# Letting the adding and the transposing transfers of a convolution and feed-forward kernel run beside each other

## The chip, the cores and the metric

One core of a Trainium2 chip runs the whole program. The metric is the device time of one execution, in microseconds (us).

## The reference, cut to what matters

Eight sequences of 4,224 tokens with 192 features pass through a convolution whose seven weights differ at each token and head, and then through a layer norm and a two-layer feed-forward net with a residual:

```
w   = softmax(weight_gen, over the 7 taps)            # per token and head (8 heads of 24 features)
y   = sum over k of w[..., k] * x[token - 6 + k]      # zeros ahead of the sequence
xn  = (y - mean(y)) / sqrt(var(y) + 1e-6) * g_ln
out = y + relu(xn @ w_ch1) @ w_ch2                    # 192 -> 768 -> 192
```

## The kernel before, in words

The tokens lie on 128 partitions and 264 columns; a column has 128 tokens, one to a partition. The work goes in chunks of four columns for the convolution (67 chunks, the first four of them otherwise) and in groups of four columns for the matrix products (66 groups).

**A chunk.** DVE multiplies x by the weights, `mul` (L544): three multiplications of two taps each into a buffer `pr` with two halves, and one of a single tap into `y`. Seven products have to be summed. Two of the six sums are left to the DMA engines: `dma_add` (L550) is issued by POOL and adds the second half of a `pr` buffer onto its first. The four others are `add` (L547) on POOL: two of them take the halves of the third buffer, and the last two, a2 and a3, take the results of the two adding transfers. There are 63 such chunks, so 126 adding transfers. Seven `pr` buffers exist, so a DVE multiplication can wait for an `add` that frees one.

**A group.** ACT sums, squares and scales the columns of `y` (L597, L602, L657) and rounds them to 16 bits (`hi`, L677). POOL makes the remainder (`lo`, L690). Both lie in one of two `hl` buffers. SP issues a transposing transfer, the *turn* (L694), into one of three `xT` buffers. PE multiplies it by the first matrix in three units of 36 matmuls (L712); each unit's result goes through ACT (`hh`, L727) and DVE (`hlo`, L729). PE then multiplies by the second matrix in two halves of 72 matmuls (L763). DVE adds the residual (L815) and SP stores (L823).

**SP's queue** also has the loads of x (L443) and of the weights (L449), and between the two output halves a step without work (the `hop`, L773) on which PE waits.

**The order.** Every operation has a place in one list, `PLACE`, written out by hand. `Plan.order` sorts by it, and each engine's instructions are issued in that order: what stands behind a waiting instruction of an engine waits too. `Plan.order` also keeps the last adding transfer and the last turn that it has met, and gives each adding transfer the last turn ahead of it as `behind`, and each turn the last adding transfer. At the end of the kernel function (L1014 to L1017) a wait is made of each `behind`: the instruction that issues the one transfer waits until the other has landed. `dma_add` waits on POOL, the turn on SP.

Of the kernel before, what the change touches and what calls it, by code (L numbers as in the profile page):

```python
# [238 lines left out]
class Plan:  # L239
# [32 lines left out]
    def order(self):  # L272
        out = sorted(self.ops, key=lambda o: o.place)
        tenant = {p: [None] * len(t) for p, t in self.pools.items()}
        done, last = set(), {"add": None, "turn": None}

        def freed(t):
            return -1 if t is None else max(x.place for x in t.ops)

        for o in out:  # L280
            assert o.deps <= done, "an operation is placed ahead of what it needs"
            for b in o.bufs:
                if b.slot is None:
                    b.slot = min(range(len(tenant[b.pool])), key=lambda i: freed(tenant[b.pool][i]))
                    assert freed(tenant[b.pool][b.slot]) < o.place, "no buffer is free"
                    tenant[b.pool][b.slot] = b
            if o.kind in last:
                o.behind, last[o.kind] = last["turn" if o.kind == "add" else "add"], o
            done.add(o)
        return out  # L290

# [2 lines left out]
def kernel(  # L294
# [30 lines left out]
    apart = mybir.DependencyInfo(mybir.DependencyClass.Sync, mybir.DependencyReason.DATA)  # L325
# [73 lines left out]
    for n in PARTS:  # L399
        pa = dict(S=s0, n=n, chunks=[], xT={})  # L400
        o = 0
# [611 lines left out]
    made = {}  # L1013
    for o in plan.order():  # L1014
        made[o] = o.fn()
        if o.behind:
            tc.add_manual_dep(made[o].ins, made[o.behind].ins.name, apart, reason="transfers kept apart")  # L1017


# [28 lines left out]
```

## Time and profile before

| | us |
|---|---|
| median of three runs | 856.57 (855.5 to 859.03) |
| the profiled execution | 856.96 |
| its span, first to last instruction | 855.2 |

PE is TensorE, PEld its weight loads, DVE VectorE, ACT ScalarE, POOL GpSimd, and SP the engine that only issues transfers. A name with q (SPq, POOLq) is the engine's sequencer, which waits and issues. In brackets at the end of a row stands the idle time ahead of an instruction and what ended it. All times in rows count from the start of the span.

### The profile page before, as it was taken

The page shows a single profiled execution, that of the slowest core. Times are in us where ns is not written, and L with a number is a line of the kernel's source. Part 1 is how long each engine was busy: PE and PEld are TensorE (multiplying, and loading weights), DVE is VectorE, ACT ScalarE, POOL GpSimd, SP SyncE. Part 2 cuts the span into 40 slices and gives each one's busy share as a digit, 9 for nine tenths or more (in the row PEclk, how much of TensorE's full clock was granted, in tenths as well). Part 3 has the DMA queues.
Part 4 walks back from the last instruction along what each step waited for, and adds up shares of the span by engine and source line. Part 5 has one row for each costly group of instructions (what it writes and reads, how often), then busy time and mean ns, then how long its engine had stood idle before and what let it go on. Part 6 is the DMA issues. An engine that isn't in the chain of part 4 may idle for free. (4 is left out here: it accounts for less than half of the span.)

```text
span 855.2 us, 37740 instructions
## 1 busy us (share of the span) xinstructions
PE 823.4 (96%) x16691; PEld 803.7 (94%) x16691; DVE 763.0 (89%) x863; ACT 646.1 (76%) x1797; POOL 728.7 (85%) x489
## 2 busy tenths in 40 slices
PE   4959999999999999999999999999999899999997
PEld 4548999999999999999999999999999899999997
DVE  7999999999999999999999999999999899673442
ACT  3888898787778888778869887878878678667521
POOL 7999999999899999999999889999986878964100
PEclk9979999999999999999999999999999999999999
DMA  9878878898878898788988799798876675845123
GB/s 219 192 176 171 166 153 186 162 199 192 188 169 198 192 190 162 181 164 189 203 187 203 163 184 197 165 168 198 190 152 151 159 137 134 158 80 108 37 74 94
DMA packets 146411, 140.91 MB, mean 165 GB/s; under 512 B 108487, under 2 KB 110415, under 8 KB 146247
## 3 DMA queue, kind: packets, MB, share of 16 engines
q1 hardware_dynamic: 127799, 88.95, 44.3%
q0 software_dynamic: 18144, 49.55, 31.3%
q8 instruction: 130, 2.13, 1.1%
q14 instruction: 34, 0.28, 0.1%
q10 hardware_dynamic: 304, 0.00, 0.0%
HBM read 36.43 MB, written 25.95 MB: 73 GB/s over the span
## 5 line engine op out<-in xcount | busy, mean ns | idle before, releaser
L547 POOL TENSOR_TENSOR y<-y,pr 128x768 f32<-128x768 f32 x252 | 514.2, 2206 | 15.4 <-DMA pr<-pr 6.1
L712 PE MATMUL ph<-xT,c_w 64*128 64x256 f16 x7128 | 417.0, 271 | 8.4 <-DVE hlo L729 8.0
L712 PEld LDWEIGHTS <-c_w 64*128 64x128 f16 x7128 | 383.8, 95 | 17.0 <-issue 11.1
L763 PE MATMUL po<-c_w2h,hh 64*128 64x192 f16 x3120 | 387.8, 243 | 0.8 <-SPq L773 0.4
L763 PE MATMUL po<-c_w2h,hlo 64*128 64x192 f16 x3120 | 387.8, 243 | 0.0
L763 PE MATMUL po<-c_w2l,hh 64*128 64x192 f16 x3120 | 387.7, 243 | 0.0
L544 DVE TENSOR_TENSOR pr<-x,wn 128x1536 f32<-128x1536 f32 (+1 forms) x193 | 332.1, 1738 | 5.5 <-POOL y L547 3.9
L763 PEld LDWEIGHTS <-hh 64*128 64x128 f16 x6240 | 307.2, 94 | 2.1 <-SPq L773 1.0
L729 DVE SCALAR_TENSOR_TENSOR hlo<-ph,hh 128x1024 f16<-128x1024 f32 x198 | 239.5, 1217 | 55.8 <-ACT hh L727 55.7
L727 ACT ACTIVATE hh<-ph 128x1024 f16<-128x1024 f32 x198 | 199.4, 1013 | 117.3 <-PE ph L712 114.8
L763 PEld LDWEIGHTS <-hlo 64*128 64x128 f16 x3120 | 175.3, 94 | 0.0
L690 POOL TENSOR_TENSOR hl<-xh,hl 128x768 f16<-128x768 f32 x66 | 132.8, 2031 | 33.3 <-ACT hl L677 33.2
L550 POOL DMA_DIRECT2D pr<-pr x126 | 130.1, 1233 | 27.4 <-DMA xT<-hl 14.4
L657 ACT ACTIVATE xh<-y,s 128x192 f32<-128x192 f32 x264 | 125.1, 535 | 22.1 <-DVE s L641 11.9
L602 ACT ACTIVATE junk<-y,s 128x192 f32<-128x192 f32 x264 | 116.1, 443 | 0.0
L597 ACT ACTIVATE junk<-y 128x192 f32<-128x192 f32 x264 | 92.2, 351 | 27.9 <-POOL y L547 27.5
L815 DVE SCALAR_TENSOR_TENSOR y<-po,c_fs,y 128x768 f32<-128x768 f32 (+1 forms) x66 | 65.7, 997 | 3.3 <-PE po L763 3.3
L544 DVE TENSOR_TENSOR y<-x,wn 128x768 f32<-128x768 f32 (+1 forms) x67 | 62.1, 933 | 0.2
L677 ACT ACTIVATE hl<-xh 128x768 f16<-128x768 f32 x66 | 55.0, 837 | 4.2 <-DMA xT<-hl 3.3
L602 ACT ACTIVATION_READ_ACCUMULATOR junk<-y,s 128x1 f32 x264 | 50.0, 189 | 0.0
L597 ACT ACTIVATION_READ_ACCUMULATOR junk<-y 128x1 f32 x264 | 49.8, 189 | 0.0
L469 POOL TENSOR_TENSOR e<-w,mx 128x672 f32<-128x672 f32 (+2 forms) x23 | 39.4, 1713 | 2.8 <-DVE mx L467 2.7
(75 smaller groups left out, 315.3 us busy)
## 6 DMA issues: line engine op xcount, KB each, us to landing
pr<-pr POOLq DMA_DIRECT2D x126, 384.0 KB, 6.2
x<-in_x_dram SPq DMA_DIRECT2D x65, 384.0 KB, 5.5
out_dram<-y SPq DMA_DIRECT2D x64, 384.0 KB, 4.4
w<-in_weight_gen_dram SPq DMA_DIRECT2D x21, 336.0 KB, 5.0
pr<-in_moe_w_ch_dram SPq DMA_DIRECT2D x2, 576.0 KB, 5.1
xT<-hl SPq DMA_TRANSPOSE x66, 3.6
hh<-in_moe_w_ch_dram SPq DMA_DIRECT2D x1, 768.0 KB, 10.1
out_dram<-y SPq DMA_DIRECT2D x4, 192.0 KB, 3.2
```

The lines of the kernel that those rows point to most:

```text
L544: E.tensor_tensor(out=ov, in0=xv, in1=wv, op=ALU.mult)
L547: Q.tensor_tensor(out=flat(0), in0=flat(0), in1=flat(k), op=ALU.add)
L550: return Q.dma_start(flat(to), flat(k), accum_op=ALU.add, max_dma_last_dim=CHUNK * D * 4)
L597: A.activation(junk[t % 2], at(y)[:, j, :], AF.Identity, scale=-1.0 / D, accum_out=at(s4)[:, 3, t : t + 1])
L602: A.activation(junk[2 + t % 2], at(y)[:, j, :], AF.Square, bias=at(s4)[:, 3, t : t + 1], accum_out=at(s4)[:, 0, t : t + 1])
L657: A.activation(paired(xh, t), at(y)[:, i, :].rearrange("p (c q) -> p c q", q=P // 2), AF.Identity, bias=at(s4)[:, 3, g + t : g + t + 1], s ...
L690: lambda xh=xh, hl=hl: Q.tensor_tensor(out=halves(hl, True), in0=pairs(xh), in1=halves(hl, False), op=ALU.subtract),
L712: T_.matmul(ph[:, r, v * 2 * P : (v + 1) * 2 * P], W["w1"][rows, WB[r][c], w, f : f + P], xv[rows, a, c, :, :], start=(v == 0 and k == 0), ...
L727: lambda: A.activation(at(hh)[:, us, :], at(ph), AF.Relu), [ph], [(hh, u)])
L729: lambda: V.scalar_tensor_tensor(out=at(hlo)[:, us, :], in0=at(ph), scalar=0.0, in1=at(hh)[:, us, :], op0=ALU.max, op1=ALU.subtract),
L763: made.append(T_.matmul(at(po)[:, z, e * D : (e + 1) * D], token(b, 2 * z + e, j)[rows], W[w][rows, j, :], start=(ph == 0 and e == 0 and k ...
L815: V.scalar_tensor_tensor(out=ysl, in0=at(po)[:, zs[0] : zs[-1] + 1, : 2 * D], scalar=W["fs"][:, 0:1], in1=ysl, op0=ALU.mult, op1=ALU.add)
```

## The change

`Plan.order` no longer records what an adding transfer or a turn stands behind, and the loop that issues the operations no longer makes a wait of it. Places, buffers, engines and all other waits stay.

```diff
-        done, last = set(), {"add": None, "turn": None}
+        done = set()
...
-            if o.kind in last:
-                o.behind, last[o.kind] = last["turn" if o.kind == "add" else "add"], o
             done.add(o)
...
         made[o] = o.fn()
-        if o.behind:
-            tc.add_manual_dep(made[o].ins, made[o.behind].ins.name, apart, reason="transfers kept apart")
```

## Rows read from the trace of the kernel before

**Rows 1.** The page, busy time of each engine over the span.
```profile
PE 823.4 (96%) x16691; PEld 803.7 (94%) x16691; DVE 763.0 (89%) x863; ACT 646.1 (76%) x1797; POOL 728.7 (85%) x489
```
**Rows 2.** Busy time by stretch (columns in the first line).
```profile
core 0: us, PE busy (x) PEld busy (x) DVE busy (x) ACT busy (x) POOL busy (x), PEclk, DMA share, GB/s
80.00:600.00 520.00, 518.27 (x10994) 512.30 (x10992) 512.24 (x560) 425.40 (x1200) 501.78 (x336) 1.00 0.85 181
...
640.00:660.00 20.00, 20.00 (x432) 20.00 (x429) 18.50 (x21) 15.80 (x46) 13.41 (x10) 1.00 0.62 134
660.00:680.00 20.00, 17.62 (x336) 16.90 (x332) 16.27 (x20) 12.27 (x32) 17.76 (x12) 0.91 0.66 154
680.00:740.00 60.00, 60.00 (x1280) 60.00 (x1278) 51.30 (x57) 47.84 (x135) 52.86 (x37) 1.00 0.73 154
740.00:760.00 20.00, 18.97 (x409) 18.76 (x405) 12.93 (x11) 13.74 (x38) 13.87 (x9) 1.00 0.49 81
```
**Rows 3.** The chain that ended last, 637 to 675 us: start, length, what.
```profile
637.86 4.70 DMA xT<-hl
642.56 0.02 issue
642.58 0.02 POOLq L550
642.60 0.50 issue
643.10 1.77 POOL pr L550 x2
644.86 1.15 POOL y L547
646.01 7.56 DMA pr<-pr
...
653.70 4.11 DMA xT<-hl
...
668.19 1.75 DVE pr L544
669.94 1.15 DVE hlo L729
671.09 0.04 issue
671.13 3.56 PE ph L712 x36
674.69 3.22 PE po L763 x72
```
**Rows 4.** The chain again, the same two pieces of PE's work later.
```profile
684.81 1.97 PE ph L712 x36
686.77 2.97 PE po L763 x72
```
**Rows 5.** Waits of SP's queue: for whom, us in total, times, longest.
```profile
SPq L694 <- DMA pr<-pr: 162.9, 34, 10.5
```
**Rows 6.** Waits of POOL over the whole span, the same columns.
```profile
POOL pr L550 <- DMA xT<-hl: 14.4, 9, 4.9
...
POOL y L547 <- DMA pr<-pr: 6.1, 8, 1.5
```
**Rows 7.** POOL in order of time, 643 to 661 us.
```profile
643.10 1.77 POOL L550 DMA_DIRECT2D pr<-pr  x2 [1.53 <-DMA xT<-hl]
644.24 2.46 POOL L547 TENSOR_TENSOR y<-y,pr 128x768 f32<-128x768 f32 x1
646.01 1.53 POOL L550 DMA_DIRECT2D pr<-pr  x1
646.79 6.39 POOL L547 TENSOR_TENSOR y<-y,pr 128x768 f32<-128x768 f32 x3
658.09 0.87 POOL L550 DMA_DIRECT2D pr<-pr  x1 [4.91 <-DMA xT<-hl]
```
**Rows 8.** DVE in order of time, the wait at 668 us.
```profile
668.19 1.75 DVE L544 TENSOR_TENSOR pr<-x,wn 128x1536 f32<-128x1536 f32 x1 [2.17 <-POOL y L547]
```
**Rows 9.** POOL in order of time, the adding transfers issued at 726 us.
```profile
725.99 3.57 POOL L550 DMA_DIRECT2D pr<-pr  x4 [1.68 <-DMA xT<-hl]
```
**Rows 10.** ACT in order of time, the wait at 745 us.
```profile
745.36 0.36 ACT L597 ACTIVATE junk<-y 128x192 f32<-128x192 f32 x1 [3.29 <-POOL y L547]
```
**Rows 11.** The turn's line, L694: time to landing.
```profile
DMA to landing us min/median/max: 3.2/3.6/6.5
```
**Rows 12.** The adding transfer's line, L550: time to landing.
```profile
DMA to landing us min/median/max: 3.8/6.2/10.7
```
**Rows 13.** Waits of PE between 80 and 855 us.
```profile
PE ph L712 <- DVE hlo L729: 4.1, 5, 2.3
PE po L763 <- SPq L773: 0.4, 1, 0.4
PE po L763 <- DVE y L815: 0.2, 1, 0.2
```
**Rows 14.** The turn's stretch on SP and its `lo` on POOL, in order of time.
```profile
645.06 0.60 SPq L823 DMA_DIRECT2D out_dram<-y  x1
653.70 1.43 SPq L694 DMA_TRANSPOSE xT<-hl  x1
...
634.41 1.97 POOL L690 TENSOR_TENSOR hl<-xh,hl 128x768 f16<-128x768 f32 x1
```

## The prediction

> **What bounds the kernel now.** I read four views in turn. The page's busy times name PE: 823.4 of 855.2 us [rows 1]. The split by stretch says when: from 80 to 600 us PE is idle 520 - 518.27 = 1.7 us, and DVE (512.24) and POOL (501.78) are nearly as full [rows 2]. So nothing that the transfers do there can give back more than 1.7 us. Of the stretches listed after that, PE has a hole in two: 20 - 17.62 = 2.4 us between 660 and 680, and 20 - 18.97 = 1.0 us between 740 and 760 [rows 2]. PE's own waits agree: 4.1 us behind DVE's `hlo`, the longest 2.3, and never for a transposed tile [rows 13]. A turn that lands earlier is therefore worth nothing to PE directly; it can only pay by way of POOL, ACT or SP.
>
> The chain of waits shows what is behind the first hole. Its links between 637 and 658 us are a turn (4.70 us), two POOL issues, an adding transfer (7.56), a turn (4.11): each transfer is issued just after the other kind has landed [rows 3]. One round of this loop is 653.70 - 637.86 = 15.8 us. PE needs for a group three units of 1.97 and two halves of 2.97 [rows 4], 11.9 us. For this round the alternation is slower than PE, while the DMA engines were busy only 0.62 of the stretch [rows 2]: it is the waiting from landing to issue that costs, not the bytes.
>
> The hole costs more than its 2.4 us. After it PE ran a unit in 3.56 us and a half in 3.22 [rows 3] where it takes 1.97 and 2.97 otherwise [rows 4]: 1.8 us more. The granted clock of that stretch reads 0.91 [rows 2], and 9% of 20 us is the same 1.8 us. Together the hole is 4.2 us.
>
> **The change, part by part.** Nothing is added and no instruction moves; two sets of waits go.
>
> *The wait of POOL's issue on a turn.* It ended 14.4 us of idle time, in 9 places [rows 6]. The two in the loop are 1.53 and 4.91 us [rows 7]. Without them POOL would be up to 6.4 us earlier at 658 us. From the end of the POOL work at 646.79 + 6.39 = 653.2 the issue at 658.09 could follow at once [rows 7]. What POOL's lateness did is in DVE's row: a multiplication stood 2.17 us for a buffer that an `add` had to free, and `hlo`, one place behind it, was the instruction that PE waited for [rows 8, 3]. 4.91 is more than twice 2.17, so I take this wait away whole, and with it PE's 2.4 us and the 1.8 us of slow clock that followed. What is late next is ACT's rounding and POOL's `lo` between the two; the margin of 4.91 - 2.17 = 2.7 us is what they may use up.
>
> *The same wait at 726 us* is 1.68 us, ahead of four issues [rows 9]. POOL is then busy until 745 us, where ACT stands 3.29 us for POOL's sum [rows 10], and PE's hole of 1.0 us follows. 1.68 covers 1.0. Here I am less sure, since PE arrives 4.2 us sooner; but ACT's and DVE's orders hold PE's evictions too, so that most of the work before this point moves forward with PE. I take 1.0.
>
> *The wait of a turn on an adding transfer.* SP stood 162.9 us in 34 of 66 turns [rows 5]. Most of this is no loss: a turn also needs its `lo`, and PE never waited for the tile [rows 13]. The turn at 653.70 shows how far one can come forward: its `lo` ended at 636.4, SP's store ahead of it was issued by 645.7 [rows 14], so it could go 8 us earlier. Behind a turn in SP's queue stand loads, stores and the hop; PE's wait on the hop is 0.4 us in all [rows 13]. I book nothing for this part. What hides it is PE's full row and the three `xT` buffers.
>
> *What the transfers cost each other.* The waits that go kept every turn of this trace apart from every adding transfer, so this price isn't in it. The nearest rows are the spreads of the times to landing, in which a transfer shares the DMA engines with others: a turn takes 3.2 to 6.5 us [rows 11], an adding one 3.8 to 10.7 [rows 12]. Per overlapped pair I bound the extra by 0 below (a gain by meeting is excluded, as both draw on the same engines) and by 6.5 - 3.2 = 3.3 us above. Who would pay? PE has no wait for a turn. POOL's `add` waited for an adding transfer in 8 places, 6.1 us [rows 6]: in these a later landing counts in full. 8 x 3.3 = 26.4 us is the upper end, against 14.4 us of waits that go. I take the lower end for the forecast, near the medians, 3.6 and 6.2, that lie close to the minima and which the loads and stores in the same queues already disturb. Both ends are kept for the range.
>
> A rule bears on this. Rows first: the DMA share was 0.85 on average from 80 to 600 us and 0.62 in the stretch of the loop [rows 2]. The Trainium skill (DMA: Bandwidth & Descriptors, Rules for kernel authors) says that transfers issued from SP, ACT and POOL run on the same 16 DMA engines and interleave, so that several issuing engines save issue time and bring no bandwidth. By that rule overlapping would only stretch each transfer, and the sum would be 0. By the rows there is idle time to fill in the loop, and the sum stays 5.2.
>
> **The sum.** 2.4 + 1.8 + 1.0 = 5.2 us off the profiled 856.96 gives **851.8 us**. The median shown is 0.4 us below the profiled execution, which I leave in the range. 0.5% of the median, about what a measurement of this kernel can tell from no change, is 4.3 us, so the limit is 852.3: the forecast is only just beyond it.
>
> **The rivals.**
>
> *No change, as the shared engines give it back* (about 855.5). The freed transfers stretch each other, POOL waits for its adding transfers where it waited for turns, and the hole at 671 us stays or moves. For it: 4.91 us of relief become 4.91 - 3.3 = 1.6 if one pair overlaps at the upper price, less than the 2.17 that DVE stood; the round is then still too long, and about 1 us of PE's idle time goes without the clock. That is the skill's rule as a mechanism. Against it: the share of 0.62. A weaker form, that the change removes waits that other waits hold anyway, is true of the 32 turns that SP did not hold back [rows 5] but not of the loop, where no other release stands within microseconds [rows 7, 14].
>
> *Slower: POOL becomes late all along* (about 863). The place is `add` a2 and a3, directly behind the landing of an adding transfer. The price is up to 3.3 us per place, in 8 places 26.4 us; less the 14.4 us freed, 12 us net. POOL is busy 501.78 of 520 us between 80 and 600 [rows 2], so it can make up little; about half would reach PE, with further drops of its clock: 857 + 6 = 863, and 869 if all does. It decides from 14.4 / 8 = 1.8 us per place on, which is below the upper price. For it: POOL's small reserve. Against it: the tight places number 8 of 126, and not each has a turn beside it.
>
> *Faster than forecast* (about 850): also the 1.7 us of 80 to 600 us go. 856.96 - 6.9 = 850.1 is the floor that PE's work allows.
>
> **How the numbers follow.** The forecast gets 0.38 and its faster neighbour 0.06, together 0.44 faster by over 0.5%. No change gets 0.33; what lies between (one hole gone, the clock's share not) belongs to it. The slower case gets 0.23. The range begins at 848.5, the floor less the 1.5 us by which runs of one kernel lie under the profiled one (855.5 against 856.96), and goes up to 863, the slower case at half pass-through, which leaves out its upper end and little else. The likeliest case alone spans 850 to 853.
>
> **What would show it.** Right: the times to landing of both kinds rise by under 2 us; POOL has no idle time behind turns, and SP none behind adding transfers; PE is busy through 660 to 680 us with the granted clock at 1.00; DVE's wait for POOL there is under 0.5 us. Wrong: POOL's `add` waits for adding transfers for over 20 us in all; or the hole returns later with another name ahead of `hlo`; or times to landing of 10 us and more become the rule.

## The result, and the profile after

The changed kernel takes 849.28 us (median of four runs, 849.1 to 851.12) against 857.56 for the kernel before (855.5 to 859.03): a ratio of 0.991, 95% interval 0.9883 to 0.9937. The profiled execution took 849.11 us, its span 847.3. The lines moved up by two: the turn is L692, the adding transfer L548, `add` L545, `lo` L688, PE's products L710 and L761.

The page's busy times, and the split by stretch (columns as in [rows 2]):

```profile
PE 819.4 (97%) x16691; PEld 802.9 (95%) x16691; DVE 762.4 (90%) x863; ACT 646.1 (76%) x1797; POOL 727.5 (86%) x489
```
```profile
80.00:600.00 520.00, 519.39 (x11044) 515.43 (x11042) 514.23 (x562) 426.67 (x1201) 503.47 (x337) 1.00 0.87 182
640.00:660.00 20.00, 20.00 (x440) 19.99 (x436) 19.50 (x27) 16.81 (x47) 15.83 (x12) 1.00 0.93 175
660.00:680.00 20.00, 20.00 (x424) 20.00 (x420) 18.66 (x19) 16.68 (x49) 17.12 (x12) 1.00 0.77 168
740.00:760.00 20.00, 20.00 (x433) 20.00 (x430) 15.29 (x13) 13.88 (x36) 11.47 (x9) 1.00 0.39 63
```

Both holes are gone, the granted clock reads 1.00 between 660 and 680 us, and in the stretch of the loop the DMA share rose from 0.62 [rows 2] to 0.93; the engines moved 175 GB/s there, where it was 134.

What POOL and SP's queue wait for now (first column who, then for whom, us in total, times, longest):

```profile
POOL pr L548 <- DVE pr L542: 13.6, 7, 4.1
...
POOL y L545 <- DMA pr<-pr: 1.6, 2, 1.1
```
```profile
SPq L692 <- POOL hl L688: 107.4, 32, 9.7
```

No issue of POOL waits for a turn any more (14.4 us in [rows 6]), and POOL's `add` stood for adding transfers for 1.6 us, not 6.1. SP's turn still waits, now for its `lo`. POOL has become early and waits for DVE instead.

Where did the time come from? PE's order is the same in both kernels, so each block of its products can be compared by its start. First PE's timeline of the kernel before, then of the changed one (start, length, engine, line, count; x72 are two units, and a block that runs past the queried stretch shows a smaller count):

```profile
661.80 4.11 PE L712 MATMUL ph<-xT,c_w 64*128 64x256 f16 x72
...
677.73 1.49 PE L712 MATMUL ph<-xT,c_w 64*128 64x256 f16 x24
...
749.95 2.28 PE L712 MATMUL ph<-xT,c_w 64*128 64x256 f16 x38 [1.03 <-DVE hlo L729]
...
850.63 0.25 PE L792 MATMUL ph<-c_w2h,hlo 128*128 128x192 f16 x1
```
```profile
659.30 4.11 PE L710 MATMUL ph<-xT,c_w 64*128 64x256 f16 x72
...
666.20 2.14 PE L710 MATMUL ph<-xT,c_w 64*128 64x256 f16 x36
...
671.14 1.05 PE L710 MATMUL ph<-xT,c_w 64*128 64x256 f16 x16
...
742.14 4.11 PE L710 MATMUL ph<-xT,c_w 64*128 64x256 f16 x72
...
842.80 0.25 PE L790 MATMUL ph<-c_w2h,hlo 128*128 128x192 f16 x1
```

At the first block PE is 661.80 - 659.30 = 2.5 us ahead, collected in steps of 0.2 to 0.6 us since 80 us; at 600 us it was 2.1. The next unit began at 671.13 before [rows 3] and at 666.20 after: 4.9 us ahead. The next block is free of the slow clock too, and starts at 671.14 where it was 677.73: 6.6 us ahead. At 749.95 against 742.14 the lead is 7.8 us, and there it stays to the end (850.63 against 842.80). So the 7.8 us are 2.5 early, 4.1 at the first hole with its clock, 1.2 at the second.

The times to landing, the turn's first, then the adding transfer's:

```profile
DMA to landing us min/median/max: 3.2/4.7/6.7
```
```profile
DMA to landing us min/median/max: 3.8/6.1/10.7
```

The median turn takes 1.1 us longer than in [rows 11]; the adding transfer takes 0.1 us less [rows 12].

### The profile page after: what moved, and what is told of

It is laid out like the page before. It is cut to its first block, busy times and chain, and to the rows that moved or that the text cites. A ratio compares the mean times of both kernels' runs of the same rounds, so it can differ in the third digit from the quotient of the medians.

```text
span 847.3 us, 37725 instructions
## 1 busy us (share of the span) xinstructions
PE 819.4 (97%) x16691; PEld 802.9 (95%) x16691; DVE 762.4 (90%) x863; ACT 646.1 (76%) x1797; POOL 727.5 (86%) x489
## 4 chain that ended last, share of the span: by engine, by line
PE 58%; DVE 10%; POOL 3%; issue 2%; ACT 1%; DMA 1%; SPq 0%; DVEq 0%; POOLq 0%
PE po L761 29%; PE ph L710 29%; DVE pr L542 5%; DVE hlo L727 3%; POOL y L545 2%; DVE y L542 1%; DVE y L813 1%; PE ph L790 1%; POOL pr L548 1%; DMA out_dram<-y 1%; ACT junk L600 0%; DVE wn L496 0%; ACT junk L595 0%; ACT hh L725 0%; POOL hl L688 0%
## 5 line engine op out<-in xcount | busy, mean ns | idle before, releaser
L545 POOL TENSOR_TENSOR y<-y,pr 128x768 f32<-128x768 f32 x252 | 505.4, 2157 | 13.9 <-DVE y L542 5.9
L710 PE MATMUL ph<-xT,c_w 64*128 64x256 f16 x7128 | 415.1, 270 | 5.0 <-DVE hlo L727 4.9
L710 PEld LDWEIGHTS <-c_w 64*128 64x128 f16 x7128 | 383.6, 94 | 11.0 <-issue 6.7
L761 PE MATMUL po<-c_w2h,hh 64*128 64x192 f16 x3120 | 387.6, 243 | 0.1
L761 PE MATMUL po<-c_w2l,hh 64*128 64x192 f16 x3120 | 387.7, 243 | 0.0
L761 PE MATMUL po<-c_w2h,hlo 64*128 64x192 f16 x3120 | 387.6, 243 | 0.0
L761 PEld LDWEIGHTS <-hh 64*128 64x128 f16 x6240 | 306.9, 94 | 0.7 <-SPq L771 0.3
L761 PEld LDWEIGHTS <-hlo 64*128 64x128 f16 x3120 | 174.9, 94 | 0.0
L688 POOL TENSOR_TENSOR hl<-xh,hl 128x768 f16<-128x768 f32 x66 | 126.7, 1938 | 40.2 <-ACT hl L675 38.1
L548 POOL DMA_DIRECT2D pr<-pr x126 | 127.7, 1194 | 15.3 <-DVE pr L542 13.6
## 6 DMA issues: line engine op xcount, KB each, us to landing
hh<-in_moe_w_ch_dram SPq DMA_DIRECT2D x1, 768.0 KB, 10.3
```

What stands on the lines that cost most here:

```text
L545: Q.tensor_tensor(out=flat(0), in0=flat(0), in1=flat(k), op=ALU.add)
L548: return Q.dma_start(flat(to), flat(k), accum_op=ALU.add, max_dma_last_dim=CHUNK * D * 4)
L688: lambda xh=xh, hl=hl: Q.tensor_tensor(out=halves(hl, True), in0=pairs(xh), in1=halves(hl, False), op=ALU.subtract),
L710: T_.matmul(ph[:, r, v * 2 * P : (v + 1) * 2 * P], W["w1"][rows, WB[r][c], w, f : f + P], xv[rows, a, c, :, :], start=(v == 0 and k == 0), ...
L761: made.append(T_.matmul(at(po)[:, z, e * D : (e + 1) * D], token(b, 2 * z + e, j)[rows], W[w][rows, j, :], start=(ph == 0 and e == 0 and k ...
```

## The experiments

The first four kernels put one part of the waits back. Each is the kernel before with one more condition at the place where the waits are made; they ran on one chip, beside 24 runs of the kernel before (median 856.23). The changed kernel ran in a job of its own; the medians of the kernel before differ by up to 1.3 us between jobs, and times compared across them are that uncertain.

**Only the turn's wait stays; POOL issues freely.**

```diff
-        if o.behind:
+        if o.behind and o.kind == "turn":
```

> The adding transfers no longer wait for turns; each turn still waits for the adding transfer ahead of it. Loop theory (the holes came from transfers that waited for each other in a ring, and cutting either side of it opens the ring): at least 5 of the 8 us come, 849 to 852 us, PE full from 660 to 680 us. Rival (POOL's 14.4 us of waits alone were the cost): the whole gain comes, 849 to 850. Second rival (the freed turns are what pays): 855 or more.

Measured: 849.34 us (849.1 to 849.46), ratio 0.9922 (0.9901 to 0.9943). The whole gain is there, though SP still stands for adding transfers and PE waits for next to nothing between 80 us and the end:

```profile
SPq L694 <- DMA pr<-pr: 122.0, 32, 10.4
```
```profile
PE ph L712 <- DVE hlo L729: 0.5, 2, 0.3
```

**Only the adding transfer's wait stays; SP issues turns freely.**

```diff
-        if o.behind:
+        if o.behind and o.kind == "add":
```

> The turns no longer wait for adding transfers; each adding transfer still waits for the turn ahead of it on POOL. Loop theory: a turn that starts up to 8 us sooner has landed before POOL asks for it, so the ring is open too and 849 to 852 us result, with under 6 us of POOL's waits on turns left of 14.4. Rival (POOL's waits alone were the cost, and they stay): 855 or more. Second rival (the freed turns are what pays): 849 to 850.

Measured: 854.37 us (853.07 to 857.52). The median is 1.9 us lower, but the ratio, 0.9992 (0.9976 to 1.0009), can't be told from no change. The loop theory fell for the whole time: it wanted 849 to 852, and under 6 us of waits. The first rival's 855 is missed by 0.6 us. POOL kept 10.3 of its 14.4 us of waits on turns. POOL's waits in total, POOL's issues in order of time up to the wait at 655 us, SP's timeline of that stretch, the time to landing of the two turns issued between 640 and 662 us, and the stretch in which the kernel before has its first hole:

```profile
POOL pr L550 <- DMA xT<-hl: 10.3, 6, 3.9
```
```profile
641.73 1.77 POOL L550 DMA_DIRECT2D pr<-pr  x2 [0.33 <-issue]
...
644.64 1.54 POOL L550 DMA_DIRECT2D pr<-pr  x1
...
655.74 0.87 POOL L550 DMA_DIRECT2D pr<-pr  x1 [3.93 <-DMA xT<-hl]
```
```profile
645.69 0.60 SPq L823 DMA_DIRECT2D out_dram<-y  x1
646.46 4.38 SPq L694 DMA_TRANSPOSE xT<-hl  x1
```
```profile
DMA to landing us min/median/max: 7.1/8.0/9.0
```
```profile
660.00:680.00 20.00, 20.00 (x433) 20.00 (x430) 18.62 (x22) 15.22 (x40) 16.70 (x11) 1.00 0.86 176
```

The turn does go 7.2 us sooner (646.46, before 653.70 [rows 14]), as soon as the store ahead of it was issued. But the adding transfers that POOL issued at 641.7 and 644.6 are in flight, and it lands after 9.0 us instead of 4.1 [rows 3]: of the 7.2 us, 4.9 are given back in flight. The other 2.3 us reach POOL, whose issue comes at 655.74 instead of 658.09 [rows 7]. With that the first hole is gone: in this execution (853.83 us) PE is full from 660 to 680 us and keeps its clock.

So the first hole is not where this kernel loses its time. It loses it in other places. At 551.84 us PE stood 1.47 us for the hop (0.45 at the same product before), after POOL's `add` had stood 2.40 us (0.58 before) for an adding transfer that took 9.6 us with a turn in flight (7.8 before). Between 680 and 740 us PE is idle for 0.5 us, and the second hole is there with 0.9 us.

**Both waits go, but only late.**

```diff
-        if o.behind:
+        if o.behind and o.place < 2168:
```

> Waits of both directions are gone from place 2168 on (from about 615 us), and stay ahead of it. If the two holes at 671 and 749 us were made by the waits beside them: 4.1 + 1.2 = 5.3 us of the 7.8 us by which PE's work ends sooner in the changed kernel come, 851.5 to 853.5 us. Rival (lateness collected before 615 us decided the holes): 855 or more.

Measured: 850.64 us (849.81 to 853.05), ratio 0.9941 (0.992 to 0.9961): 1.4 us over the fully changed kernel, and 1.3 over the one above in which POOL issues freely. In its profiled execution PE is busy for the whole of 660 to 680 and of 740 to 760 us, so most of the gain belongs to the waits beside the holes. The time is 0.9 us below the expected range; the early waits cost 1.4 us here and not the 2.5 us of the profiled pair.

**Both waits go, but only early.**

```diff
-        if o.behind:
+        if o.behind and o.place >= 2168:
```

> Waits of both directions are gone up to place 2167 (about 615 us), and stay from there on. If the holes were made by the waits beside them, both stay and only the 2.2 us come by which PE was ahead at 621 us in the changed kernel: 854.5 to 856. Rival (lateness collected before decided the holes): the first hole goes with them, 850 to 852.

Measured: 853.4 us (851.93 to 856.72), ratio 0.9976 (0.996 to 0.9993). This lies between the two expectations. The second hole stays, with 0.9 us of idle time between 740 and 760 us. Of the first, little is left:

```profile
660.00:680.00 20.00, 19.53 (x410) 19.14 (x406) 17.84 (x18) 14.96 (x42) 15.72 (x11) 1.00 0.68 163
```

PE is idle 0.5 us here, not 2.4 [rows 2], and keeps its clock. Nor is it the same place: the unit that had to wait at 671.13 us before starts at 666.94 without a wait, and PE stands 0.42 us two units later, at 679.60. So lateness from before 615 us counts: without it, the waits of the loop no longer make the first hole. By the kernel with late waits freed, lateness without these waits doesn't make it either. The two gains, 5.6 us there and 2.8 here in the same job, add up to more than the 6.9 us of the kernel in which POOL issues freely, as they would if each takes the first hole away.

**The waits put back for the loop alone.**

```diff
-        if o.behind:
+        if o.behind and 2168 <= o.place <= 2330:
```

> The changed kernel with the waits of both directions put back for the transfers at places 2168 to 2330 alone (some 615 to 670 us), 13 of 192. If POOL's waits on turns there make the first hole: it comes back, 851 to 854 us, with POOL idle behind turns for 3 to 8 us. Rival (the hole needs the lateness of the waits before it too): 849 to 850, no change from the changed kernel.

Measured: 852.57 us (850.69 to 855.35, ten runs; before 856.66 in the same job), ratio 0.9954 (0.9936 to 0.9973). The waits of these transfers (15 by the list, ten adding ones and five turns, not the 13 that the expectation names) cost 3.3 us over the changed kernel by the medians. The profiled execution is the fastest of the ten, and in it POOL has two waits on turns there, 7.6 us, within the expected 3 to 8. POOL's two issues and, below them, the stretch of the first hole:

```profile
653.89 0.88 POOL L550 DMA_DIRECT2D pr<-pr  x1 [4.79 <-DMA xT<-hl]
...
666.78 0.88 POOL L550 DMA_DIRECT2D pr<-pr  x1 [2.80 <-DMA xT<-hl]
```
```profile
660.00:680.00 20.00, 19.53 (x410) 19.14 (x406) 17.83 (x18) 14.55 (x40) 15.32 (x10) 1.00 0.78 165
```

The hole itself did not come back as expected, though. As with the early waits freed, PE doesn't wait at the unit of 671.13 us (666.95 here) and stands 0.42 us two units later, with its clock kept. This execution took 850.69 us, 1.9 less than the median, and what PE did in the other nine isn't known. The second hole, beside which no wait was put back, is gone (20.00 of 20 us between 740 and 760).

**No wait, but POOL made late by other work.** The changed kernel with memsets of a scratch tile, which nobody reads, ahead of five adding transfers:

```diff
     made = {}
+    late = {2195: 2, 2238: 1, 2292: 5, 2502: 2, 2565: 1}
     for o in plan.order():
+        for _ in range(late.get(o.place, 0)):
+            Q.memset(scratch, 0.0)
         made[o] = o.fn()
```

> The changed kernel, without any wait between the two kinds, but with memsets of a scratch tile on POOL (about 1 us each, 11 in all) ahead of five adding transfers at which POOL had stood for turns in the kernel before (places 2195, 2238, 2292, 2502, 2565; 10.7 us there). If POOL's lateness in itself makes the holes, whoever makes it late: they come back in part, 851 to 855 us. Rival (the hole needs transfers that meet or wait): 849 to 850.

Measured: 853.92 us (852.91 to 855.51), ratio 0.9961 (0.9935 to 0.9988): 4.6 us over the changed kernel. POOL's timeline, PE's, and the stretch of the first hole:

```profile
650.15 5.53 POOL L1016 MEMSET scratch<- 128x1152 f32 x5
655.62 0.88 POOL L549 DMA_DIRECT2D pr<-pr  x1
```
```profile
668.69 2.14 PE L711 MATMUL ph<-xT,c_w 64*128 64x256 f16 x36 [1.85 <-DVE hlo L728]
```
```profile
660.00:680.00 20.00, 18.02 (x376) 17.66 (x372) 16.13 (x15) 12.92 (x36) 15.54 (x11) 1.00 0.97 163
```

The hole is back at the same unit, ended by the same `hlo`, and no transfer had waited for one of the other kind. DVE stood 2.5 us for POOL's `add` on the way, as it did before for 2.17 [rows 8]. The slow clock did not come back: PE was idle for 2.0 us and the granted clock reads 1.00.

So it is POOL's lateness that makes the hole, whatever makes POOL late. The profiled executions also say how late: what counts is POOL's issue (the one at 658.09 us before) against PE's own progress, for which the start of PE's block at 661.80 us can stand.

| kernel | POOL's issue, us | PE's block, us | issue ahead of block | PE stands at the next unit |
|---|---|---|---|---|
| before | 658.09 | 661.80 | 3.7 | 2.26 |
| changed, with memsets | 655.62 | 659.76 | 4.1 | 1.85 |
| waits in the loop alone | 653.89 | 660.01 | 6.1 | 0 |
| only early waits gone | 653.88 | 660.01 | 6.1 | 0 |
| only SP free | 655.74 | 662.14 | 6.4 | 0 |
| changed | 648.09 | 659.30 | 11.2 | 0 |

The memsets bring POOL's issue 0.4 us earlier against PE than before, and the hole is 0.4 us shorter; where the issue is 2.4 us earlier or more, there is no hole at this unit. A wait of 4.8 us in the loop shows at PE or not, by how late POOL already is.

**The price of meeting, by itself.** A kernel of transfers alone, of the sizes and forms used here, run once: ten rounds each of the five combinations, each round behind the landing of the one before. In its text the combinations are:

```python
((add_alone,), (turn_alone,), (add_first, add_second), (add_beside, turn_beside_one),
 (add_first_beside, add_second_beside, turn_beside_two))
```

> No convolution and no feed-forward: ten rounds each of an adding transfer alone, a turn alone, two adding transfers, an adding transfer beside a turn, and two beside a turn, each round behind the landing of the one before; one tile is stored. The times to landing are what counts. If the engines interleave and share: beside one another each takes 1 to 2 us longer than alone (adding about 4, turn about 3.2 us alone). Rival (the transfers fit beside each other at no price): within 0.3 us of alone. Third way (the transposing one is held up far more): over 6.5 us for the turn.

Times to landing of the single rounds, in this order: adding alone, turn alone, adding beside a turn, the turn beside it.

```profile
DMA to landing us min/median/max: 3.9/3.9/4.1
...
DMA to landing us min/median/max: 3.6/3.7/3.7
...
DMA to landing us min/median/max: 5.2/5.7/5.8
...
DMA to landing us min/median/max: 4.7/5.3/5.8
```

And of the rounds with two adding transfers: the first and the second without a turn, the first and the second beside a turn, and that turn.

```profile
DMA to landing us min/median/max: 3.9/3.9/4.0
...
DMA to landing us min/median/max: 5.5/5.5/5.5
...
DMA to landing us min/median/max: 5.2/5.2/5.6
...
DMA to landing us min/median/max: 6.7/6.7/7.0
...
DMA to landing us min/median/max: 4.8/5.1/5.5
```

By the medians each kind pays 1.2 to 1.8 us for the other: 5.7 - 3.9 and 5.3 - 3.7 in the pair; 5.2 - 3.9, 6.7 - 5.5 and 5.1 - 3.7 in the three. It is the first of the three ways expected. The price is for bare pairs and threes; with the kernel's other transfers about, the one freed turn above paid 4.9 us (9.0 against 4.1). Still, one behind the other a pair lands after 3.9 + 3.7 = 7.6 us, and beside each other both are there after 5.7.

## Why the prediction was right, point by point

**The holes: right in place and size, and in the cause with one thing missing.** 4.2 us were booked for the first with its clock, 4.1 came; 1.0 for the second, 1.2 came. That POOL's lateness makes them is shown from two sides: without its waits on turns they go though the turns still wait, and with memsets in their place both return (2.0 us idle at the first, 0.9 at the second). What the prediction left out is the lateness that POOL brings into the loop: with the wait of 4.8 us put back in the loop and no waits ahead of it, PE did not stand at that unit in the profiled execution. And the 1.8 us of slow clock, booked as a consequence of the hole, followed it in the profiled execution of the kernel before alone; the hole of 2.0 us under memsets came with the granted clock at 1.00. How often the clock's part is lost isn't known. The signs listed for "right" are in the trace: the median landings rose by 1.1 us at most, POOL has no wait for turns, PE and its clock are full, and DVE's wait for POOL of 2.17 us [rows 8] has gone from that stretch. The sign for SP holds too, though it says nothing: SP's wait moved to `lo`, and it can stay on the adding transfers at no cost.

**The turn's wait booked at nothing: right.** With POOL free, 122.0 of SP's 162.9 us of waits on adding transfers [rows 5] are left, and keeping or dropping them gives 849.34 or 849.28 us.

**The term that was mis-sized: the stretch from 80 to 600 us.** It was booked at 0, and its bound of 1.7 us was taken from PE's busy time. In the profiled pair PE was 2.1 us ahead at 600 us and 2.5 at 661, and that is most of why the measured 849.11 lies below the predicted floor of 850.1. The bound was wrong as a bound. The record of one product is some 270 ns long (the page's mean for L710), while a unit starts a pair of them every 1.97 / 18 = 0.11 us [rows 4]; a stall shorter than the difference, 0.16 us, leaves no gap between the records, and a longer one shows that much too short. At the two holes this can be read off: gaps of 2.26 and 1.03 us cost PE 2.4 and 1.2. The records of the weight loads are short (94 ns on the page) and show it: PEld was idle 520 - 512.30 = 7.7 us there [rows 2], 520 - 515.43 = 4.6 now, 3.1 less. The row to take for the bound stood next to the one that was taken; as it fell by 3.1 where PE's work came 2.1 sooner, it bounds a gain and doesn't size it. The Trainium skill (Trainium Kernel Development and Optimization, Performance Expectations) says this of matmul busy time, that pipelining makes it a bad measure and that the share of weight loads is a good one; this trace agrees.

**The upper price of 3.3 us per meeting: too high for a bare pair.** The price kernel shows 1.2 to 1.8, and the changed kernel's median turn 1.1; but it was no bound, as the one freed turn that paid 4.9 us shows. What excluded the slower rival is more than the price, though. Its point of decision was put at 1.8 us in 8 places, and 1.8 is just reached; but POOL's waits for adding transfers fell from 6.1 to 1.6 us, though turns and adding transfers now meet. The likely reason, which no run tested alone, is that an adding transfer that no longer waits for a turn is issued sooner, and that this outweighs the meeting; with memsets to delay the issues, the same waits were 5.1 us. The rival counted the meetings and left the earlier start out.

**The rule of the shared engines** (the Trainium skill, DMA: Bandwidth & Descriptors, Rules for kernel authors) was weighed as the case for no change. The price kernel agrees that the transfers share: each takes longer beside the other. The conclusion, a sum of 0, didn't hold: beside each other a pair is done 7.6 - 5.7 = 1.9 us sooner than in series, and in the stretch of the loop the DMA share had room to rise from 0.62 to 0.93. Where the stretching does show is the kernel with freed turns alone: there 4.9 of the 7.2 us of one turn's earlier start went in flight, and one adding transfer's landing came late enough for PE to stand at 551 us.

**A reading that fell in between.** The prediction described the loop as transfers that wait for each other in a ring, and the expectations took from it that cutting either side would do. For the first hole of the profiled executions either side did. For the whole time only POOL's side did, 849.34 against 854.37 us. A wait on POOL holds up everything behind it in POOL's order, four `add`s to a chunk with DVE's buffers behind them. A wait on SP holds up loads, stores, the hop and a tile that PE never waited for [rows 13]; PE did stand for the hop once, 0.4 us, and then SP's turn had been waiting for POOL's `lo`.

**The number.** 849.28 us lies outside the 850 to 853 us that the prediction called likeliest, and 0.8 us inside its range. The lower end of that range was set for the scatter of runs and not for more gain, and the excess over the forecast came from the early stretch. It is in part luck that the range holds 849.28.

**Left open.** Which of the early waits give the small steps before 661 us isn't settled. The largest, 0.6 us, is the one at 551 us where PE had stood for the hop; it is gone as well in the profiled execution of the kernel that keeps the early waits. That kernel put the early waits at 1.4 us, the profiled pair at 2.5, and runs of the kernel before spread by more than the difference.

## What to carry to other kernels

When two engines wait for each other's transfers, ask what is queued behind each wait: 122 us of waits left on one queue cost nothing here, and dropping the 14 us on the other brought the whole gain. Whether one such wait shows at the bounding engine depends on how late the waiting engine already is, so look at the lateness ahead of a wait as well as at its length. Bound a stretch that looks full by the shortest records in it, since long pipelined ones cover short stalls. A transfer that is freed to start sooner lands sooner by less if it then meets others (2.3 of 7.2 us here); free the one whose landing nobody stands for, or free the one who stands.

## What was not expected of the hardware

The kernels in which POOL never stands for a turn scatter little: 849.1 to 849.46 us over six runs with POOL free, against 852.91 to 858.97 for the kernel before over 24 runs of the same job. In a second job the kernel before took 853.01 to 865.67 us over 19 runs. Each of the four kernels that keep some of POOL's waits on turns spread over 3 to 5 us, also the one in which only the loop's are held (850.69 to 855.35). The fully changed kernel (849.1 to 851.12) and the one with memsets (852.91 to 855.51) lie between. Why the waits bring scatter as well as time wasn't tried.
